# Splits of stored weight sums in place, and a changed order of small preparation jobs, in a fused attention and two-MLP kernel

## The chip, the core and the metric

The kernel runs as one program on one core of a Trainium2 chip. The metric is the device time of one execution in microseconds (us). Three timed runs of the kernel before gave 981.01, 981.85 and 983.27 us; the median is 981.85 us.

## The reference

```
scores = scale * q @ k^T - slope_h * |i - j|, masked to 0 <= i - j < 128
attn   = exp(scores - max) / (sum + 1e-9);  x = attn @ v        # 4 x 8 heads, 576 x 64
h = x @ w_in;  g = h * clip(h + 3, 0, 6) / 6;  x = g @ w_out    # 2304 x 512, 2048 features
xn = x / sqrt(mean(x^2) + 1e-6) * rms_g                         # second MLP, 1536 features
out = (silu(xn @ w_gate) * (xn @ w_val)) @ w_out2
```

The attention inputs and the output are float32. The weights are float64; the kernel gets them as 64-bit words and makes float32 of them itself.

## The kernel before, in words

Every float32 matrix is split into a rounded high part and the low rest, and a product is three matmuls (high by high, high by low, low by high). ScalarE (ACT) makes the high part with a copy, VectorE (DVE) the low part with a subtraction. A split is therefore an ACT instruction, then a DVE instruction that waits for it, and where the parts go to memory two stores.

The program has two halves. In the first (to about 533 us) attention and the first MLP run together in 6 blocks of 3 token tiles, 16 feature chunks each. Alongside, `Second.turn` (L269) converts the second MLP's weights in 36 turns, in the order of `TURNS` (L65): kinds 0 and 1 are the gate and value weights of a chunk, kind 2 is the output weight, of which each pair of chunks also gives two sums that go to memory as `sum32`, still unsplit.

In the second half 36 groups follow (`group`, L913): group i works on tokens of pair i // 12 and feature chunk i % 12. A group forms gate and value of its chunk by a scheme with seven products of six matmuls each, `product(0)` to `product(6)`, into three PSUM banks `ps_1`, `ps_6`, `ps_5`. Between them stand small instructions that read a bank before the next product may add to it:

- L938: ACT copies the first product to `s1`. `product(2)` adds to that bank, and waits until the copy is done.
- L941: DVE adds `s1` and `ps_6`. `product(3)` adds to `ps_6`, and waits for it.
- L944: ACT's silu of `ps_1`, after `product(2)`.
- L947: DVE adds `s1` and `ps_6` again; `product(5)` starts anew in `ps_6`, and waits for it.
- L950, L952, L956, L957: DVE's last adds and the multiplication.

Engines run their instructions in program order, with waits for each other. What is not part of a group's own chain is put between these by tables: `job(i, slot, ...)` hangs a piece of work on group i at a slot ("start" before `product(0)`, "silu" behind L944, "sum", "silu 2" behind the second silu, "end" behind L957, and numbers 0 to 5 behind the units of the output product that follow the group).

Groups 0 to 11 multiply their result by the output weights directly (`outputs`, L971, after groups 2, 4, 6, 8, 11 and 12). Groups 12 to 35 form six rounds of four groups. A round's output product is again one with seven factors (`Round`, L1038): its units run after groups 5, 6 and 7 counted from the round's first, so after groups 17, 18, 19 for round 0 (`phase`, L1121). DVE adds each unit's result to a total (L1135; in the first round of a token pair ACT copies it for some units, L1133). A unit of the names in `CHAINED` adds to the bank of an earlier unit, and waits until that unit's result was read. The operands of a round, B11, B12, B21, B22 and the sums T1 to T4 of the two chunk pairs p = 0 and 1, are made by `sum` (DVE, L1078), `high` (ACT, L1081) and `low` (DVE, L1084), where `ROUND_JOBS` (L75) says; the key is (group counted from the round's end, slot). `FINAL_JOBS` (L96) does it for the last round, which has no groups behind it.

The round's other factors are sums of output weights. `load_sum` (L301) loads one `sum32` piece of 128x512 into `ws`, `split_sum` (L305) splits it, and two stores put the parts back (L311); `Round.fetch` loads them as `u` (L1097) three factors ahead. Loads and stores, and `tw`, the operands of a later group (L889, two of 896 KB each at a group's end), are issued by the one queue of SyncE (SP), which waits in order.

The jobs of the pair of tokens after (`x.scale`, `x.later`, `x.high`, `x.low` in `turn`, L1176) go through the same slots.

Of the kernel before, what the change touches and what calls it, by code (L numbers as in the profile page):

```python
# [10 lines left out]
F32 = mybir.dt.float32  # L11
F32R = mybir.dt.float32r
# [8 lines left out]
P = 128  # L21
# [35 lines left out]
B11, T2, B21, T3, T1, T4, B22 = range(7)  # L57
# [4 lines left out]
PAIRS2 = NTILE // 6  # L62

ROUND = 4
TURNS = [(m + i, k) for m in range(0, M2, 2) for i, k in ((0, 2), (0, 0), (1, 2), (0, 1), (1, 0), (1, 1))]  # L65
FACTORS = {"c": ("S4", "B22"), "g": ("S3", "T3"), "a": ("A11", "B11"), "b": ("A12", "B21"), "e": ("S1", "T1"), "f": ("S2", "T2"), "d": ("A22", "T4")}
SEQUENCE = list(FACTORS)
STORED = {"A11": (0, 0, 0), "A12": (0, 1, 0), "A22": (0, 1, 1), "S2": (1, 0, 0), "S3": (1, 0, 1), "S4": (1, 1, 0), "S1": (1, 1, 1)}
ADDED_TO = {"c": "C12", "a": "V", "g": "C22", "b": "C11", "e": "V", "f": "V", "d": "Z"}
SUMMED = ["C11", "C12", "C22", "V", "Z"]  # L70
BLOCK_RING = (12, 10, 11)
SPLIT_AT = 5
OPERANDS = "B22 B11 B21 T3 T1 T2 T4".split()
CHAINED = {"b": "a", "d": "e"}
ROUND_JOBS = {  # L75
    (-1, "silu"): [("high", "B22", 0)],
    (-1, "silu 2"): [("low", "B22", 0)],
    (-1, 2): [("high", "B11", 0)],
    (-1, 3): [("low", "B11", 0)],
    (-1, 5): [("sum", "T1", 0)],  # L80
    (0, "start"): [("high", "B11", 1), ("high", "B22", 1), ("low", "B11", 1), ("sum", "T1", 1)],
    (0, "silu"): [("sum", "T3", 0), ("sum", "T3", 1), ("low", "B22", 1), ("high", "T3", 0), ("high", "T3", 1)],
    (0, "silu 2"): [("high", "B21", 0), ("high", "B21", 1)],
    (0, "end"): [("low", "T3", 0)],
    (1, "start"): [("low", "T3", 1)],
    (1, "silu"): [("sum", "T2", 0), ("sum", "T2", 1), ("low", "B21", 0)],
    (1, "silu 2"): [("low", "B21", 1)],
    (1, 2): [("high", "T1", 0), ("high", "T1", 1)],
    (1, 3): [("high", "T2", 0), ("high", "T2", 1), ("low", "T1", 0)],
    (2, "start"): [("low", "T1", 1), ("sum", "T4", 0)],  # L90
    (2, "silu"): [("low", "T2", 0), ("low", "T2", 1)],
    (2, "silu 2"): [("sum", "T4", 1)],
    (2, 3): [("high", "T4", 0), ("high", "T4", 1)],
    (3, "start"): [("low", "T4", 0), ("low", "T4", 1)],
}
FINAL_JOBS = {  # L96
    (-2, "start"): [("high", "B11", 0), ("high", "B21", 0), ("high", "B22", 0)],
    (-2, "silu"): [("low", "B11", 0)],
    (-2, "silu 2"): [("low", "B21", 0), ("low", "B22", 0)],
    (-2, "end"): [("sum", "T1", 0), ("sum", "T3", 0)],  # L100
    (-2, 3): [("sum", "T2", 0), ("sum", "T4", 0), ("high", "T3", 0), ("high", "T2", 0)],
    (-1, "silu"): [("low", "T3", 0), ("low", "T2", 0), ("high", "T1", 0), ("high", "T4", 0)],
    (-1, "silu 2"): [("low", "T1", 0)],
    (-1, "end"): [("low", "T4", 0), ("high", "B11", 1), ("high", "B21", 1), ("high", "B22", 1)],
# [8 lines left out]
}  # L113
UNITS = {5: "c0 c1 g0 g1".split(), 6: "a0 a1 b0 b1".split(), 7: "e0 e1 f0 f1 d0 d1".split()}

# [5 lines left out]
def f32(ap):  # L121
    return ap.bitcast(F32)
# [3 lines left out]
def fused_kernel(ctx: ExitStack, tc: tile.TileContext, qd, kd, v, w1, w2, rms_g, out, out_t):  # L126
# [7 lines left out]
    vec, act, pool, pe, sp = nc.vector, nc.scalar, nc.gpsimd, nc.tensor, nc.sync  # L134
# [105 lines left out]
    class Second:  # L240
# [109 lines left out]
    W1, W2 = First(), Second()  # L350
# [177 lines left out]
    def at(t):  # L528
        return [slots[kind].get(t, []) for kind in KINDS]
# [128 lines left out]
    for t in range(AHEAD):  # L658
        q, s_, d_, t_, _, v_ = at(t)
# [105 lines left out]
    for p, (b, m0, m1) in enumerate(PARTS):  # L765
# [3 lines left out]
        if p == 2:  # L769
            conv.close()  # L770
            ypool = ys.enter_context(tc.tile_pool(name="ypool", bufs=3, **OPEN))
        if last:
# [3 lines left out]
            ypool = p2.enter_context(tc.tile_pool(name="ypool2", bufs=3, **OPEN))  # L776
# [3 lines left out]
        for m in range(m0, m1):  # L780
# [48 lines left out]
            if p == 0:  # L829
                k = m + 1  # L830
# [18 lines left out]
            if last:  # L849
# [6 lines left out]
                for x in early:  # L856
                    k = m - EARLY[x.m]
# [48 lines left out]
    def job(i, at, f, *args):  # L906
        jobs.setdefault((i, at), []).append((f, args))
# [130 lines left out]
    class Round:  # L1038
# [70 lines left out]
        def plan(self, job):  # L1109

            i = self.i0 + ROUND
            if self.final:
                for at, jobs_ in FINAL_JOBS.items():
                    for f, *args in jobs_:
                        job(i + at[0], at[1], getattr(self, f), *args)
                return
            for at, jobs_ in ROUND_JOBS.items():
                for f, *args in jobs_:
                    job(i + at[0], "end" if self.r == 0 and at[0] < 0 and at[1] != "silu" else at[1], getattr(self, f), *args)
# [40 lines left out]
    for m, x in parts.items():  # L1160
        i = m - 2
# [14 lines left out]
    def turn(s):  # L1176

        i, x = s * M2, Inputs(s + 1)
        job(i + 5, "start", x.load)
        if s:  # L1180
            for c in range(KC):
                job(i + 6, ("silu", "end")[c // 2], x.scale, c, act)
            job(i + 7, "silu", x.later, "S1", 0)
            job(i + 7, 2, x.later, "S2", 1)
            job(i + 7, 2, x.high, 0)
            job(i + 7, 4, x.low, 0)
            job(i + 9, 3, x.later, "S4", 2)
            job(i + 9, 3, x.high, 1)
            job(i + 10, "silu 2", x.low, 1)
            job(i + 10, 3, x.later, "S3", 3)  # L1190
            for k in range(2, 7):
                job(i + 11, {2: "silu", 3: "sum", 5: "silu 2"}.get(k, "end"), x.high, k)
                job(i + 11, k - 1, x.low, k)
# [17 lines left out]
    for i in range(M2):  # L1211
        job(SPLIT_AT - 1 + i, "end", W2.load_sum, i)
        job(SPLIT_AT + i, "silu", W2.split_sum, i)

    for i in range(M2 * PAIRS2):
        s, m = divmod(i, M2)
# [17 lines left out]
        x = Round.all.get(i - ROUND)  # L1234
# [4 lines left out]
    x = rounds[-1]  # L1239
# [48 lines left out]
```

## Time and profile before

| | |
|---|---|
| timed runs | 981.01, 981.85, 983.27 us |
| the profiled execution | 985.32 us, its span 983.6 us |
| mean granted TensorE clock | 0.983 of full speed |
| busy: PE, DVE, ACT, POOL | 943.7, 696.0, 479.2, 220.4 us |
| DMA | 197.08 MB, mean 200 GB/s |

PE (TensorE) is busy for 96% of the span, so PE's idle stretches, and stretches at a lower granted clock, are what another order of the work can change. In the chain of work that ended last PE has 78%, DVE 10%, ACT 5% and DMA 3%.

The views used below: the timeline lists an engine's instructions with start, duration, line and tile, and in brackets the idle time before the first of them and what ended it. The chain goes from the end back to what released each step. The windows give busy time of PE, PEld, DVE, ACT and POOL in a stretch, then the granted clock, DMA share and GB/s.

### The profile page before, as it was taken

The page shows a single profiled execution, that of the slowest core. Times are in us where ns is not written, and L with a number is a line of the kernel's source. Part 1 is how long each engine was busy: PE and PEld are TensorE (multiplying, and loading weights), DVE is VectorE, ACT ScalarE, POOL GpSimd, SP SyncE. Part 2 cuts the span into 40 slices and gives each one's busy share as a digit, 9 for nine tenths or more (in the row PEclk, how much of TensorE's full clock was granted, in tenths as well). Part 3 has the DMA queues.
Part 4 walks back from the last instruction along what each step waited for, and adds up shares of the span by engine and source line. Part 5 has one row for each costly group of instructions (what it writes and reads, how often), then busy time and mean ns, then how long its engine had stood idle before and what let it go on. Part 6 is the DMA issues. An engine that isn't in the chain of part 4 may idle for free.

```text
span 983.6 us, 15380 instructions
## 1 busy us (share of the span) xinstructions
PE 943.7 (96%) x5408; PEld 845.7 (86%) x5408; DVE 696.0 (71%) x1464; ACT 479.2 (49%) x1049; POOL 220.4 (22%) x359
## 2 busy tenths in 40 slices
PE   7899999999999999999999997999989999999997
PEld 4577888888888888888899996889879998999986
DVE  5788666555888787876576664788465778685776
ACT  6799556355556556553454442433135333223420
POOL 4333013233334533433331332100000000020001
PEclk8899999999999999999999998999999999999999
DMA  6445411114775655542466778787979666777616
GB/s 234 175 182 197 172 38 31 41 52 129 241 235 179 204 184 171 199 161 93 143 230 218 269 249 308 257 291 254 310 283 339 233 236 214 251 267 253 230 53 207
DMA packets 96044, 197.08 MB, mean 200 GB/s; under 512 B 7008, under 2 KB 67424, under 8 KB 92768
## 3 DMA queue, kind: packets, MB, share of 16 engines
q1 hardware_dynamic: 95968, 196.11, 57.8%
q8 instruction: 42, 0.69, 0.3%
q14 instruction: 34, 0.28, 0.1%
HBM read 142.61 MB, written 53.48 MB: 199 GB/s over the span
## 4 chain that ended last, share of the span: by engine, by line
PE 78%; DVE 10%; ACT 5%; DMA 3%; issue 2%; POOL 1%; SPq 0%; ACTq 0%; DVEq 0%; POOLq 0%
PE ps_o L578 18%; PE ps_h L565 18%; PE ps_o L930 8%; PE ps_S L930 7%; PE ps_y L1104 7%; PE ps_A L930 5%; PE ps_y L980 5%; DMA ws<-s 3%; PE ps_av L499 3%; PE ps_h L930 3%; PE ps_t L481 2%; PE ps_s L438 2%; PE ps_s L429 1%; DVE wx L195 1%; ACT wx L188 1%
## 5 line engine op out<-in xcount | busy, mean ns | idle before, releaser
L578 PE MATMUL ps_o<-w,g 128*128 128x512 f32 x864 | 224.0, 402 | 2.1 <-DVE w L199 1.9
L565 PE MATMUL ps_h<-xs,w 128*128 128x384 f32 x1152 | 220.6, 339 | 0.0
L565 PEld LDWEIGHTS ps_h<-xs,w 128*128 128x128 f32 x1152 | 202.1, 188 | 6.7 <-DVE t L805 1.2
L578 PEld LDWEIGHTS ps_o<-w,g 128*128 128x128 f32 x864 | 156.2, 188 | 41.0 <-issue 6.1
L805 DVE SCALAR_TENSOR_TENSOR t<-t,ps_h 128x384 f32<-128x384 f32 x96 | 53.0, 552 | 87.2 <-ACT t L804 87.2
L804 ACT ACTIVATE t<-ps_h,three 128x384 f32<-128x384 f32 x96 | 55.5, 578 | 80.9 <-PE ps_h L565 74.7
L1104 PE MATMUL ps_y<-u 128*128 128x384 f32 x432 | 84.7, 337 | 1.9 <-DVE u L1135 1.7
L1151 POOL TENSOR_TENSOR u<-u 128x384 f32<-128x384 f32 x6 | 7.2, 1237 | 332.3 <-DVE u L1135 332.3
L1104 PEld LDWEIGHTS ps_y<-u 128*128 128x128 f32 x432 | 76.2, 189 | 2.9 <-DVE u L1135 2.5
L467 ACT ACTIVATE t<-t,m 128x128 f32<-128x128 f32 (+1 forms) x144 | 61.1, 426 | 29.4 <-DVE t L459 15.8
L810 ACT CAST g<-t 128x384 fp32r<-128x384 f32 x96 | 49.3, 514 | 53.2 <-DVE t L805 51.7
L816 DVE TENSOR_TENSOR g<-t,g 128x384 fp32r<-128x384 f32 x96 | 55.8, 581 | 23.1 <-ACT g L810 22.2
L953 ACT ACTIVATE r<-r 128x384 f32<-128x384 f32 x36 | 18.9, 526 | 106.0 <-DVE r L952 106.0
L469 POOL TENSOR_SCALAR r<-den 128x2 f32<-128x2 f32 x72 | 27.8, 387 | 182.8 <-ACT t L467 181.0
L930 PE MATMUL ps_o<-S,tw 128*128 128x384 f32 x336 | 66.7, 340 | 0.3 <-DVE t L950 0.3
L930 PEld LDWEIGHTS ps_o<-S,tw 128*128 128x128 f32 x336 | 58.9, 188 | 2.4 <-DVE u L941 1.6
L470 POOL TENSOR_TENSOR r<-r,minus 128x2 f32<-128x2 f32 x72 | 56.0, 778 | 6.0
L488 POOL TENSOR_SCALAR_AFFINE_SELECT pt<-pt 128x256 f32<-128x256 f32 x82 | 39.7, 487 | 76.6 <-ACT pt L486 73.7
L980 PE MATMUL ps_y<-wo,g 128*128 128x512 f32 x216 | 50.8, 394 | 0.0
L980 PEld LDWEIGHTS ps_y<-wo,g 128*128 128x128 f32 x216 | 41.3, 192 | 8.3
L452 DVE CUSTOM_DVE_ANT_0 t<-ps_s,rel 128x256 f32<-128x256 f32 (+2 forms) x128 | 45.1, 393 | 4.4 <-PE ps_s L438 4.4
L1081 ACT CAST u<-u 128x384 fp32r<-128x384 f32 x66 | 32.1, 512 | 30.2 <-DVE u L1078 14.3
(168 smaller groups left out, 1765.6 us busy)
## 6 DMA issues: line engine op xcount, KB each, us to landing
tw<-t SPq DMA_DIRECT2D x52, 896.0 KB, 6.5
wraw<-w SPq DMA_DIRECT2D x36, 512.0 KB, 4.3
wraw<-w SPq DMA_DIRECT2D x16, 1024.0 KB, 8.9
u<-s SPq DMA_DIRECT2D x48, 256.0 KB, 5.9
t<-th SPq DMA_DIRECT2D x12, 896.0 KB, 4.5
t<-tl SPq DMA_DIRECT2D x12, 896.0 KB, 4.3
u<-w SPq DMA_DIRECT2D x36, 256.0 KB, 5.4
w<-w SPq DMA_DIRECT2D x12, 512.0 KB, 2.9
```

Source lines behind the costliest of these rows:

```text
L452: vec.tensor_tensor_reduce(out=self.t[:, a, c0:], in0=s[:, c0:], in1=(rel_split if self.i in SPLITS else rel)[:, c0:], scale=2.0 ** (-8.0 ...
L467: act.activation(p, p, AF.Exp, bias=self.m[:, a : a + 1], scale=-1.0, accum_out=self.den[:, a : a + 1])
L470: pool.tensor_tensor(self.r, self.r, minus, ALU.pow)
L565: pe.matmul(ps[:, : n * P], lhsT=w[:, a, c * P : (c + 1) * P], rhs=xs[c][:, b, : n * P], start=(k == 0), stop=(k == 3 * KC - 1),)
L578: pe.matmul(o, lhsT=g[:, a, i * P : (i + 1) * P], rhs=w[:, b], start=(m == first and a == 0 and b == 0), stop=(m == last and a == 1),)
L804: act.activation(r[:, :nq], ps[:, :nq], AF.Relu, bias=three)
L805: vec.scalar_tensor_tensor(out=r[:, :nq], in0=r[:, :nq], scalar=6.0, in1=ps[:, :nq], op0=ALU.min, op1=ALU.mult)
L810: act.copy(g[:, 0, :nq], r[:, :nq])
L816: vec.tensor_sub(g[:, 1, :nq], r[:, :nq], f32(g[:, 0, :nq]))
L930: pe.matmul(ps, lhsT=w[a][:, k, c * P : (c + 1) * P], rhs=x[:, b, c], start=(start and j == 0), stop=(j == 5), skip_group_check=True,)
L980: pe.matmul(ps, lhsT=gs[i + k][:, a, t // 3, t % 3 * P : (t % 3 + 1) * P], rhs=wo[i + k][:, b], start=(k == 0 and a == 0 and b == 0), stop ...
L1104: pe.matmul(ps, lhsT=w[:, p, a, d * P : (d + 1) * P], rhs=self.part(name, p, b), start=(p == j == 0 and k not in CHAINED), stop=(p == 1 an ...
```

## The change

The order of turns differs for chunks 4, 5 and 8, 9. A weight sum is loaded at the start of the group before its split (it was at that group's end), into one of two fixed pairs of tiles, and the low part overwrites the loaded piece. The splits stand in groups 7 to 10 and 12 to 19 (they stood in groups 5 to 16). Most jobs of a round and of the last round stand at other slots.

```diff
-TURNS = [(m + i, k) for m in range(0, M2, 2) for i, k in ((0, 2), (0, 0), (1, 2), (0, 1), (1, 0), (1, 1))]
+TURN_ORDER = ((0, 2), (0, 0), (1, 2), (0, 1), (1, 0), (1, 1)), ((0, 0), (0, 1), (0, 2), (1, 0), (1, 2), (1, 1))
+TURNS = [(m + i, k) for m in range(0, M2, 2) for i, k in TURN_ORDER[m in (4, 8)]]
-SPLIT_AT = 5
+SPLIT_AT = (7, 8, 9, 10, 12, 13, 14, 15, 16, 17, 18, 19)
 ROUND_JOBS = {
...
-    (-1, 5): [("sum", "T1", 0)],
-    (0, "start"): [("high", "B11", 1), ("high", "B22", 1), ("low", "B11", 1), ("sum", "T1", 1)],
+    (-1, 5): [("sum", "T3", 0), ("high", "T3", 0)],
+    (0, "start"): [("high", "B11", 1), ("high", "B22", 1), ("sum", "T2", 0)],
...
 FINAL_JOBS = {
...
-    (-2, "silu 2"): [("low", "B21", 0), ("low", "B22", 0)],
-    (-2, "end"): [("sum", "T1", 0), ("sum", "T3", 0)],
+    (-2, "silu 2"): [("low", "B11", 0)],
...
         def load_sum(self, i):
-            self.late[i] = ypool.tile([P, DM], F32, tag="y", name="ws")
-            sp.dma_start(out=self.late[i], in_=self.sum32[i // 2][:, i % 2])
+            k = i % 2
+            if k not in self.late:
+                self.late[k] = tuple(
+                    ypool.tile([P, DM], F32, tag=tag, name=name, bufs=1 if tag == "yt" else 3)
+                    for tag, name in (("y", "ws"), ("yt" if k else "y", "wt"))
+                )
+            sp.dma_start(out=self.late[k][0], in_=self.sum32[i // 2][:, k])

         def split_sum(self, i):
-            x = self.late.pop(i)
-            high, low = (ypool.tile([P, DM], F32R, tag="y", name="wt") for _ in range(2))
-            act.copy(high, x)
-            vec.tensor_sub(low, x, f32(high))
-            for k, y in enumerate((high, low)):
-                sp.dma_start(out=self.sums[i // 2][:, i % 2, k], in_=f32(y))
+            x, high = self.late[i % 2]
+            act.copy(high.bitcast(F32R), x)
+            vec.tensor_sub(x.bitcast(F32R), x, high)
+            for k, y in enumerate((high, x)):
+                sp.dma_start(out=self.sums[i // 2][:, i % 2, k], in_=y)
...
-    job(SPLIT_AT - 1 + i, "end", W2.load_sum, i)
-    job(SPLIT_AT + i, "silu", W2.split_sum, i)
+    job(at_ - 1, "start", W2.load_sum, i)
+    job(at_, "silu", W2.split_sum, i)
```

Every engine has as many instructions as before, and PE's are in the same order. Three places show what moves. The first is SP's queue around groups 13 and 14, before:

```order
L1097 DMA u<-w_1_130 128x2x256
L311 DMA s_4_139<-wt 128x512 x2
L303 DMA ws<-s_4_145 128x512
L889 DMA tw<-t_121 128x1792 x2
L311 DMA s_4_139<-wt 128x512 x2
L303 DMA ws<-s_5_146 128x512
L889 DMA tw<-t_122 128x1792 x2
```

and of the change, where `ws` is a load, `s<-wt` and `s<-ws` the stores of a split:

```order
L1109 DMA u<-w_1_130 128x2x256
L316 DMA ws<-s_3_144 128x512
L323 DMA s_2_137<-wt 128x512
L323 DMA s_2_137<-ws 128x512
L901 DMA tw<-t_121 128x1792 x2
L316 DMA ws<-s_3_144 128x512
L323 DMA s_3_138<-wt 128x512
L323 DMA s_3_138<-ws 128x512
L901 DMA tw<-t_122 128x1792 x2
```

The load stood between a group's stores and its `tw` pair. It now stands behind the `tw` pair of the group before and ahead of the stores.

The second is ACT around the start of group 24 (first group of a round), before; `u` and `S` rows of L1081 are `high` pieces, the `s` row is the copy of the first product:

```order
L754 CAST S_8554<-sums 128x768
L1081 CAST u<-u 128x384 x2
L1081 CAST S_7175<-u 128x384
L938 COPY s_8623<-ps_h 128x384
L944 ACTIVATE r<-ps_h 128x384
L1081 CAST u<-u 128x384 x2
```

and of the change (12 is added to the line numbers):

```order
L766 CAST S_8524<-sums 128x768
L1093 CAST u<-u 128x384 x3
L1093 CAST S_7155<-u 128x384
L950 COPY s_8593<-ps_h 128x384
L956 ACTIVATE r<-ps_h 128x384
L965 ACTIVATE r<-r 128x384
```

One more `high`, that of T3 for p = 0, stands ahead of the copy. The same holds at the starts of groups 16, 20, 28 and 32.

The third is DVE at the end of group 34, before; the L1078 rows are sums, L1084 `low` pieces, L1135 the adds of the units' results:

```order
L952 TENSOR_TENSOR r<-u,ps_A 128x384
L1078 TENSOR_TENSOR u<-u 128x384
L1084 TENSOR_TENSOR u<-u 128x384 x2
L956 TENSOR_TENSOR u<-u,ps_S_9616 128x384
L957 TENSOR_TENSOR u<-u,r 128x768
L1078 TENSOR_TENSOR u<-u 128x384 x2
L1135 TENSOR_TENSOR u<-u,ps_y 128x384 x4
```

and of the change:

```order
L964 TENSOR_TENSOR r<-u,ps_A 128x384
L1096 TENSOR_TENSOR u<-u 128x384
L968 TENSOR_TENSOR u<-u,ps_S_9584 128x384
L969 TENSOR_TENSOR u<-u,r 128x768
L1147 TENSOR_TENSOR u<-u,ps_y 128x384 x3
```

Four of the five jobs between L952 and the first L1135 stand elsewhere.

## Rows read from the trace of the kernel before

**Rows 1.** PE's timeline, second half (one row first half): waits stand in brackets
```profile
611.12 1.01 PE L930 MATMUL ps_A<-A,th 128*128 128x384 f32 x2 [6.52 <-DVE u L947]
640.01 0.69 PE L930 MATMUL ps_A<-A,th 128*128 128x384 f32 x2 [2.49 <-DVE u L947]
689.20 1.32 PE L930 MATMUL ps_A<-A,tw 128*128 128x384 f32 x6 [0.17 <-DVE u L947]
714.29 1.33 PE L930 MATMUL ps_A<-A,tw 128*128 128x384 f32 x6 [1.44 <-DVE u L947]
727.52 1.33 PE L930 MATMUL ps_h<-A,tw 128*128 128x384 f32 x6 [0.54 <-ACT s L938]
729.65 1.32 PE L930 MATMUL ps_A<-S,tw 128*128 128x384 f32 x6 [0.80 <-DVE u L941]
823.73 1.47 PE L930 MATMUL ps_A<-S,tw 128*128 128x384 f32 x6 [1.97 <-DVE u L941]
944.16 0.68 PE L1104 MATMUL ps_y<-A,u 128*128 128x384 f32 x1 [1.96 <-DVE u L1135]
963.73 8.62 PE L1104 MATMUL ps_y<-u 128*128 128x384 f32 x48 [1.74 <-DVE u L1135]
322.20 0.44 PE L481 MATMUL ps_t<-ident,t 128*128 128x128 f32 x2 [0.48 <-ACT pt L486]
```

**Rows 2.** The chain of waits around group 6: start, duration, what
```profile
597.89 11.28 DMA ws<-s
...
611.12 2.29 PE ps_A L930 x6
613.41 1.92 PE ps_S L930 x6
615.33 8.83 PE ps_y L980 x36
```

**Rows 3.** The same chain elsewhere: paces at full and at lower clock
```profile
582.61 8.18 PE ps_y L980 x36
...
640.01 1.97 PE ps_A L930 x6
641.99 1.92 PE ps_S L930 x6
...
734.18 2.10 PE ps_S L930 x12
...
944.16 3.92 PE ps_y L1104 x12
```

**Rows 4.** Windows of 10 us; granted clock is the third number from the end
```profile
610.00:620.00 10.00, 8.88 (x31) 7.95 (x32) 6.11 (x9) 5.97 (x8) 2.88 (x4) 0.67 0.49 171
710.00:720.00 10.00, 8.56 (x49) 8.24 (x48) 4.67 (x8) 2.26 (x5) 0.00 (x0) 1.00 0.97 350
820.00:830.00 10.00, 8.03 (x37) 7.71 (x37) 6.93 (x14) 2.38 (x6) 0.00 (x0) 0.83 0.30 101
```

**Rows 5.** ACT's timeline in group 8 and at the start of group 20
```profile
638.15 0.62 ACT L308 CAST wt<-ws 128x512 fp32r<-128x512 f32 x1 [1.28 <-DMA ws<-s]
773.05 0.93 ACT L1081 CAST u<-u 128x384 fp32r<-128x384 f32 x2
```

**Rows 6.** DVE's timeline at the starts of groups 16, 24 and 28
```profile
725.58 0.96 DVE L957 TENSOR_TENSOR u<-u,r 128x768 f32<-128x768 f32 x1
820.26 0.55 DVE L1135 TENSOR_TENSOR u<-u,ps_y 128x384 f32<-128x384 f32 x1
869.66 1.25 DVE L1078 TENSOR_TENSOR u<-u 128x384 f32<-128x384 f32 x1
```

**Rows 7.** DMA issues, 530 to 760 us: count, KB each, median us to landing
```profile
tw<-t SPq DMA_DIRECT2D x24, 896.0 KB, 6.9
s<-wt SPq DMA_DIRECT2D x24, 256.0 KB, 4.2
ws<-s SPq DMA_DIRECT2D x12, 256.0 KB, 4.9
```

More of the change, by code (lines that the diff above doesn't have):

```diff
@@ L75 @@
 ROUND_JOBS = {
-    (-1, "silu"): [("high", "B22", 0)],
-    (-1, "silu 2"): [("low", "B22", 0)],
+    (-1, "start"): [("high", "B22", 0)],
+    (-1, "silu"): [("low", "B22", 0)],
     (-1, 2): [("high", "B11", 0)],
     (-1, 3): [("low", "B11", 0)],
-    (-1, 5): [("sum", "T1", 0)],
-    (0, "start"): [("high", "B11", 1), ("high", "B22", 1), ("low", "B11", 1), ("sum", "T1", 1)],
-    (0, "silu"): [("sum", "T3", 0), ("sum", "T3", 1), ("low", "B22", 1), ("high", "T3", 0), ("high", "T3", 1)],
-    (0, "silu 2"): [("high", "B21", 0), ("high", "B21", 1)],
+    (-1, 4): [("sum", "T1", 0)],
+    (-1, 5): [("sum", "T3", 0), ("high", "T3", 0)],
+    (0, "start"): [("high", "B11", 1), ("high", "B22", 1), ("sum", "T2", 0)],
+    (0, "silu"): [("low", "B11", 1), ("sum", "T1", 1), ("low", "B22", 1)],
+    (0, "silu 2"): [("sum", "T3", 1), ("high", "T3", 1)],
     (0, "end"): [("low", "T3", 0)],
-    (1, "start"): [("low", "T3", 1)],
-    (1, "silu"): [("sum", "T2", 0), ("sum", "T2", 1), ("low", "B21", 0)],
+    (1, "start"): [("sum", "T2", 1), ("high", "B21", 0), ("high", "B21", 1)],
+    (1, "silu"): [("low", "T3", 1), ("low", "B21", 0)],
     (1, "silu 2"): [("low", "B21", 1)],
+    (1, "end"): [("sum", "T4", 0)],
+    (1, 0): [("sum", "T4", 1)],
     (1, 2): [("high", "T1", 0), ("high", "T1", 1)],
-    (1, 3): [("high", "T2", 0), ("high", "T2", 1), ("low", "T1", 0)],
-    (2, "start"): [("low", "T1", 1), ("sum", "T4", 0)],
+    (1, 3): [("low", "T1", 0)],
+    (2, "start"): [("low", "T1", 1), ("high", "T2", 0), ("high", "T2", 1)],
     (2, "silu"): [("low", "T2", 0), ("low", "T2", 1)],
-    (2, "silu 2"): [("sum", "T4", 1)],
     (2, 3): [("high", "T4", 0), ("high", "T4", 1)],
@@ L97 @@
     (-2, "start"): [("high", "B11", 0), ("high", "B21", 0), ("high", "B22", 0)],
-    (-2, "silu"): [("low", "B11", 0)],
-    (-2, "silu 2"): [("low", "B21", 0), ("low", "B22", 0)],
-    (-2, "end"): [("sum", "T1", 0), ("sum", "T3", 0)],
[L101 to L104, printed above, removed]
[8 rows of a table removed]
+    (-2, "silu 2"): [("low", "B11", 0)],
+    (-2, 2): [("low", "B21", 0)],
+    (-2, 3): [("low", "B22", 0), ("sum", "T1", 0)],
+    (-1, "silu"): [("sum", "T3", 0), ("sum", "T2", 0), ("sum", "T4", 0), ("high", "T3", 0)],
+    (-1, "silu 2"): [("low", "T3", 0)],
+    (-1, "end"): [("high", "B11", 1), ("high", "B21", 1), ("high", "B22", 1)],
+    (-1, 0): [("low", "B11", 1)],
+    (-1, 1): [("low", "B21", 1)],
+    (-1, 2): [("low", "B22", 1)],
+    (-1, 3): [("sum", "T1", 1)],
+    (-1, 4): [("sum", "T3", 1), ("high", "T3", 1)],
+    (-1, 5): [("sum", "T2", 1)],
+    (2, 1): [("low", "T3", 1), ("high", "T1", 0), ("high", "T1", 1)],
+    (2, 2): [("sum", "T4", 1)],
+    (2, 3): [("low", "T1", 0), ("high", "T2", 0), ("high", "T2", 1)],
+    (1, 0): [("low", "T1", 1)],
+    (1, 1): [("low", "T2", 0)],
+    (1, 2): [("low", "T2", 1), ("high", "T4", 0), ("high", "T4", 1)],
+    (1, 3): [("low", "T4", 0)],
+    (3, 0): [("low", "T4", 1)],
 }
@@ L1118, in plan @@
                 for f, *args in jobs_:
-                    job(i + at[0], "end" if self.r == 0 and at[0] < 0 and at[1] != "silu" else at[1], getattr(self, f), *args)
+                    job(i + at[0], {2: "silu", 3: "silu", 4: "silu 2", 5: "end"}.get(at[1], at[1]) if self.r == 0 and at[0] < 0 else at[1], getattr(self, f), *args)
         def phase(self, off, by):
@@ L1192, in turn @@
                 job(i + 11, {2: "silu", 3: "sum", 5: "silu 2"}.get(k, "end"), x.high, k)
-                job(i + 11, k - 1, x.low, k)
+                job(i + 11, {2: "silu 2", 3: "end"}.get(k, k - 3), x.low, k)
             return
@@ L1210, in fused_kernel @@
         x.plan(job)
-    for i in range(M2):
-        job(SPLIT_AT - 1 + i, "end", W2.load_sum, i)
-        job(SPLIT_AT + i, "silu", W2.split_sum, i)
+    for i, at_ in enumerate(SPLIT_AT):
+        job(at_ - 1, "start", W2.load_sum, i)
+        job(at_, "silu", W2.split_sum, i)
     for i in range(M2 * PAIRS2):
```

8 rows, old and new, of the table FINAL_JOBS are left out of this document.

## The prediction

> **What bounds the kernel now.** I read the page's busy shares first: PE is busy for 943.7 of 983.6 us. PE's program is the same after the change, so the change can only take away or add PE's idle stretches, and stretches at a lower clock. Next I read who PE waits for, and then PE's timeline [rows 1], where the reader is to see that the waits of the second half fall into three sorts. One is L947 behind a split of a weight sum: 6.52 us in group 6, 2.49 in group 8, 1.44 in group 14. One is the first group of a round (0.54 and 0.80 in group 16, 1.97 in group 24). One is the last round (1.96 after group 34, 1.74 after group 35). The chain [rows 2] shows what lies behind the first: the load of a weight sum takes 11.28 us to land, ACT's copy waits for it, DVE's subtraction waits for ACT, and L947 stands behind that subtraction in DVE's order. The windows [rows 4] show what follows a long wait: the granted clock of the window with the 6.52 us is 0.67, of the one with the 1.97 us 0.83, that is time at 1.2 instead of 2.4 GHz; with the 1.44 us it is 1.00. The price is in the chain: twelve matmuls after the 6.52 us take 2.29 + 1.92 us [rows 2], at full clock 2.10 [rows 3].
>
> **The splits of the weight sums.** No instruction is added: a split is still one ACT copy, one DVE subtraction of the same shape and two stores. The load moves from a group's end to its start.
> - Group 6 has no split any more. The wait of 6.52 goes, the slow twelve matmuls give back 2.29 + 1.92 - 2.10 = 2.11, the slow output product 8.83 - 8.18 = 0.65 [rows 2, 3]. Sum 9.28.
> - Group 8 keeps a split. Of its 2.49 us only the 1.28 that ACT waited for the load goes [rows 5]; the rest is ACT's larger copy ahead of the split, which stays. A wait of 1.21 is shorter than the 1.44 that kept the full clock [rows 1, 4], so the slow stretch goes too: 1.97 + 1.92 - 2.10 = 1.79 [rows 3]. Sum 3.07.
> - Group 14: 1.44 less the 0.17 that a split costs PE even when its load is there [rows 1]. Sum 1.27.
> - Groups 17, 18 and 19 get a split that they did not have: 3 x 0.17 = 0.5 lost.
>
> What is late next? The load now stands behind the `tw` pair in SP's queue, and it overwrites a tile whose two stores must have landed. In the short groups 13 to 16 a group takes 12 + 30 matmuls, 7.35 us at the pace of [rows 3] (2.10 for 12). The split comes after three products of the next group and L944, some 3.5 us into it, so the load has about 10.9 us from the start of its group. Against that stand the `tw` pair's landing of 6.9 us and, for the reused tile, stores that take 4.2 us to land [rows 7] and leave about 3 us before the start. The load should land 8 to 9 us after the start: in time, with little to spare, so I charge 0.7 us. Behind a load that waits for stores stand the stores of the next split and then the next `tw` pair; `tw` is needed two groups, 14.7 us, after its request and lands in 6.9, so a delay of a few us there is hidden. The parts are fetched for round 0 behind group 12, and the splits that it needs end in group 10, so the later splits cost nothing. The part as a whole: 9.28 + 3.07 + 1.27 - 0.5 - 0.7 = 12.4 us gained. From the other side, were every load as late as before, only group 6 would gain.
>
> Here the Trainium skill speaks against the change (DMA: Bandwidth & Descriptors, section "Queues, rings and completion order"): descriptors are consumed in ring order, so a load issued behind two 896 KB transfers starts behind them. By its peak of 436 GB/s the pair alone would take 4.2 us, an estimate from that page; the trace has 6.9 us to landing [rows 7]. By that rule the load loses its place at the front, and that is the first rival below.
>
> **The rounds.** DVE loses work at the starts: ahead of L941 the T2 sum stands in place of a `low` and the T1 sum. But ACT gets one more `high`, that of T3, ahead of the copy `s1` for which `product(2)` waits, and this `high` waits for a DVE sum that was only just placed behind the last add of the phase. A `high` takes 0.41 us in a row (two in 0.93, less the tail) [rows 5], `s1` 0.48.
> - Group 16: L957 ends at 725.58 + 0.96 = 726.54 [rows 6]. The T3 sum follows (0.47), then three `high` (1.24) and `s1` (0.48) with some 0.1 of signals: 728.8. `product(2)` was ready at 727.52 - 0.54 = 726.98 [rows 1]. Wait 1.85 against 0.54 + 0.80 now: 0.5 lost.
> - Group 24: DVE is behind here. Its last add of the phase starts at 820.26 [rows 6]. In the new order one `low` of the next operands (0.95, of which 0.87 until the next) and the T1 sum (0.47) come ahead of it and one copy's rest (0.58) leaves, so 821.0; the T3 sum ends at 822.0, and three `high` and `s1` give 823.8. `product(3)` could have started at 823.73 - 1.97 = 821.76 [rows 1], `product(2)` one product (1.05) earlier, at 820.7. Wait 3.1 against 1.97: 1.1 lost.
> - Group 28: the sum runs beside GpSimd there and takes up to 1.25 instead of 0.55 [rows 6]; a wait of 1.0 to 1.7 in place of one of that size: 0.1 lost.
> - Groups 20 and 32 (ACT copies the last units itself, the DVE sum is early): one more `high`, 0.41 less a slack of 0.3: 0.1 to 0.2 each; the B22 `high` ahead of `s1` in 19 and 31 likewise 0.1 each. Together 0.5.
> - Clock: the waits of groups 16 and 24 lie at or above those followed by a slow stretch; group 24 has one already [rows 4]. I charge a third of 1.79 for group 16: 0.6.
> Sum: 0.5 + 1.1 + 0.1 + 0.5 + 0.6 = 2.8 lost. Bounds: nothing lost and the 0.54, 0.80 and half of 1.97 gained (2.3), or each of the five starts as bad as group 24 (below).
>
> On group 28 the Trainium skill (SBUF — State Buffer, "Who interferes with whom") says that a VectorE instruction with two SBUF inputs and a GpSimd instruction that reads SBUF block each other for whole instructions. The sum is of that kind, and 1.25 us against 0.55 agrees. [...]
>
> **The last round.** After group 34 the unit b waits for the add of unit a, which waits for DVE: five jobs stand between L952 and that add, and four of them leave. L956 then starts when PE's product ends, L957 after it (0.96 [rows 6]), the add ends about 2.3 us after the product, and the third unit can start after 2.10 [rows 3]: a wait of about 0.25 instead of 1.96. Gain 1.7, and the slow twelve matmuls 3.92 - 2.10 = 1.82 [rows 3]. After group 35 each add has one job beside it now (0.47 + 0.47 per unit of 1.05), so DVE keeps up and the 1.74 goes. Sum 5.3. Later units need their operands at least three units after the jobs, so nothing is late there. Bounds: 1.96 + 1.82 + 1.74 = 5.5 gained; or, if a job lands one unit late twice, 2.1 less.
>
> **The turns** move instructions in the first half only. PE has two waits there that hang on them (the first stands in [rows 1], 0.48, the other is under 0.7). A conversion of kind 2 stays in that place, so I take 0, bounds plus and minus 1.2.
>
> **The sum.** 12.4 - 2.8 + 5.3 = 14.9 us. Against the profiled execution of 985.32 us that is 970.4; that one is 3.5 us above the median, and against the median of 981.85 it is 967.0 us.
>
> **Rivals.**
> 1. The loads stay late, since they stand behind `tw` and wait for stores. For it: the DMA share is 0.97 in the window of group 14 [rows 4]. Against it: the request comes over 2 us earlier even after the stores. Then groups 13 to 16 wait 1.3 us each as group 14 did (5.2) and group 8 keeps its slow stretch (1.8): 974.0.
> 2. Slower side: the `high` of T3 ahead of `s1` decides at all five starts. It needs DVE to be as far behind at each as in group 24; for it, ACT's order; against it, DVE has gaps before the others. Each start then costs 3.1 plus a slow stretch of 1.8 to 2.8 as after 6.52 us, 4.9 to 5.9; five are 24.5 to 29.5, less today's 5.1 (0.54, 0.80, 1.97, 1.79): 19.4 to 24.4 in place of 2.8. The time is 983.6 to 988.6. It decides from 4.6 us per start.
> 3. The load that lands after 11.28 us belongs to the profiled execution, which is 3.5 us longer than the median. Then 3.5 less is gained: 970.5.
> 4. Those heads of rounds hide in PE's running ahead, and the T3 cost is nought: 962 to 964.
>
> **How the numbers follow.** Forecast 0.55, rival 1 0.15, rival 2 0.05, rival 3 0.10, rival 4 0.12, unknown 0.03. The range reaches from rival 4, with 3 us for the turns and what I did not see, to rival 1, with 2 more: 959 to 976. About 0.2% (2 us) is what a measurement can tell. Faster 0.93, same 0.03, slower 0.04.
>
> **What would show it.** Right: no wait at L947 over 0.6 us but in group 8, ACT not waiting for `ws`, no slow stretch near groups 6, 8 and 34, and a wait of PE for ACT's `s1` at groups 16, 24 and 28 that was 0.54 us at one place before. Wrong: ACT waits for `ws` in groups 13 to 16, waits for `s1` over 3 us at more than one round, or new waits for `tw`.

## The result, and the profile after

The changed kernel takes 970.8 us (median of 6 runs, 969.73 to 974.01); the kernel before took 982.66 us beside it (6 runs, 981.01 to 986.07). The ratio is 0.9879, interval 0.9856 to 0.9902: 11.9 us, or 1.2%, faster. The forecast was 967.0 us in a range of 959 to 976.

The profiled execution took 970.52 us (span 968.8, mean clock 0.992); before it was 985.32 us. PE is busy for 937.8 us in place of 943.7. PE's timeline after, at the places of [rows 1], start, duration, what, and in brackets the wait:

```profile
628.19 0.63 PE L942 MATMUL ps_A<-A,th 128*128 128x384 f32 x2 [2.04 <-DVE u L959]
700.91 1.32 PE L942 MATMUL ps_A<-A,tw 128*128 128x384 f32 x6 [0.17 <-DVE u L959]
715.42 1.32 PE L942 MATMUL ps_h<-A,tw 128*128 128x384 f32 x6 [1.84 <-ACT s L950]
752.49 1.32 PE L942 MATMUL ps_o<-A,tw 128*128 128x384 f32 x6 [1.03 <-DVE u L959]
764.12 1.32 PE L942 MATMUL ps_h<-A,tw 128*128 128x384 f32 x6 [0.92 <-ACT s L950]
812.52 1.83 PE L942 MATMUL ps_h<-A,tw 128*128 128x384 f32 x6 [3.09 <-ACT s L950]
860.38 1.32 PE L942 MATMUL ps_h<-A,tw 128*128 128x384 f32 x6 [1.31 <-ACT s L950]
```

The 6.52 us of group 6 and both waits of the last round (1.96 and 1.74) have no row any more. Behind groups 34 and 35 the output products now begin and run on without a wait in brackets:

```profile
932.90 0.44 PE L1116 MATMUL ps_y<-A,u 128*128 128x384 f32 x1
942.59 14.73 PE L1116 MATMUL ps_y<-u 128*128 128x384 f32 x84
```

What is left of waits over 0.6 us is that of group 8 (2.49 before) and five at the starts of rounds and in group 19, four of them for ACT's copy `s1`. The list of waits (430 to 970 us; who waits for whom: us in total, times, longest) puts that copy on top:

```profile
PE ps_h L942 <- ACT s L950: 7.3, 5, 3.1
PE ps_A L942 <- DVE u L959: 2.7, 5, 2.0
PE ps_o L942 <- DVE u L959: 2.0, 4, 1.0
```

To lay the two traces side by side I took the start of `s1` in each group (the COPY rows `s<-ps` of ACT) and added up the stretches, in us (the first relu is ACT's first instruction on a result of the first MLP):

| stretch | before | changed | difference | foretold |
|---|---|---|---|---|
| start to the first relu | 42.79 | 40.38 | -2.4 | 0 |
| first relu to group 4 (turns) | 533.59 | 534.42 | +0.8 | 0 |
| group 4 to 15 (splits) | 141.43 | 129.62 | -11.8 | -12.9 |
| group 15 to 34 (rounds, splits in 17 to 19) | 216.22 | 220.25 | +4.0 | +3.3 |
| group 34 to PE's end (last round) | 44.90 | 39.46 | -5.4 | -5.3 |

The profiled difference of 14.8 us meets the foretold 14.9 by chance: 2.4 us of it lie before the first relu, where both programs have the same instructions in the same order. In a second profile of the changed kernel (below) and in those of its variants this stretch took 40.4 to 42.3 us; what sets it is open. From the first relu on the difference is 12.4, which agrees with the 11.9 that the runs give.

### The profile page after: what moved, and what is told of

It is laid out like the page before. It is cut to its first block, busy times and chain, and to the rows that moved or that the text cites. A ratio compares the mean times of both kernels' runs of the same rounds, so it can differ in the third digit from the quotient of the medians.

```text
span 968.8 us, 15365 instructions
## 1 busy us (share of the span) xinstructions
PE 937.8 (97%) x5408; PEld 840.3 (87%) x5408; DVE 692.6 (71%) x1464; ACT 478.5 (49%) x1049; POOL 217.4 (22%) x359
## 4 chain that ended last, share of the span: by engine, by line
PE 73%; DVE 11%; ACT 7%; DMA 4%; issue 3%; POOL 2%; SPq 0%; ACTq 0%; POOLq 0%; DVEq 0%
PE ps_o L590 18%; PE ps_h L577 18%; PE ps_o L942 8%; PE ps_S L942 6%; PE ps_y L1116 5%; PE ps_A L942 4%; PE ps_y L992 4%; PE ps_h L942 3%; PE ps_av L511 2%; DMA tx<-b 2%; DMA tw<-t 1%; PE ps_t L493 1%; DVE u L1147 1%; ACT t L479 1%; DVE wx L203 1%
## 5 line engine op out<-in xcount | busy, mean ns | idle before, releaser
L479 ACT ACTIVATE t<-t,m 128x128 f32<-128x128 f32 (+1 forms) x144 | 61.2, 426 | 29.4 <-DVE t L471 14.9
L500 POOL TENSOR_SCALAR_AFFINE_SELECT pt<-pt 128x256 f32<-128x256 f32 x82 | 36.9, 452 | 81.9 <-ACT pt L498 79.0
```

Of the source, the lines that this page charges most:

```text
L479: act.activation(p, p, AF.Exp, bias=self.m[:, a : a + 1], scale=-1.0, accum_out=self.den[:, a : a + 1])
```

## The experiments

Tables give stretches as above, from one profile of each kernel; times and ratios are those of the timed runs, each against runs of the kernel before on the same chip.

### The four parts alone

**Splits.** The kernel before with `load_sum`, `split_sum`, `SPLIT_AT` and the two jobs of the change, and nothing else of it:

```diff
+    job(at_ - 1, "start", W2.load_sum, i)
+    job(at_, "silu", W2.split_sum, i)
```

> The kernel before with the in-place splits, the earlier loads and the new places of the splits alone. My theory: the stretch from group 5 to 7 gets 9.3 to 9.8 us shorter, group 8 only about 0.5 us (its larger ACT copy waits for GpSimd's sums of a tile that DMA brings late, in place of the load), group 14 about 1.3 us, group 19 loses 0.9 us because a DVE sum of the next tokens stands behind the split. In all 10 to 11.5 us faster, 971 to 972.5. Rival (the loads stay late behind the two large transfers): ACT waits for the loaded piece in groups 13 to 16, about 1.3 us each, and the gain is 5 to 7 us.

Measured: 973.54 us (4 runs), ratio 0.9893 (0.9873 to 0.9913). From the first relu on the profile is 9.9 us shorter: group 4 to 15 is 13.4 shorter, group 15 to 34 2.5 longer, 2.1 of it in groups 18 and 19, and the stretch behind group 34 1.2 longer, where this kernel has no edit. Group 8 is 2.0 us shorter and not 0.5, since no slow stretch follows its wait here. So the splits carry most of the result, and the ones put into 17 to 19 cost five times the 0.5 that I had charged.

**Rounds.** Only `ROUND_JOBS` and what hangs on it:

```diff
+    (-1, 5): [("sum", "T3", 0), ("high", "T3", 0)],
+    (0, "start"): [("high", "B11", 1), ("high", "B22", 1), ("sum", "T2", 0)],
```

> The kernel before with the new places of a round's jobs alone (and of the pair's low parts in group 23). My theory: PE waits for ACT's copy of the first product at the starts of groups 16, 20, 24 and 28, about 1.8, 0.9, 3.1 and 1.3 us, in place of waits at L941 and one of 0.54; in all 2 to 4 us slower than before. Rival (the spread of the sums pays): the waits at L941 go and nothing takes their place, 3 to 5 us faster.

Measured: 984.73 us (10 runs), ratio 1.0015 (0.9999 to 1.003). Group 15 to 34 is 3.2 us longer, group 34 to the end 2.1 shorter. There T4's sum has left the place in front of the chained unit, which takes the wait of 1.96 us to 1.50:

```profile
943.89 0.44 PE L1106 MATMUL ps_y<-A,u 128*128 128x384 f32 x1 [1.50 <-DVE u L1137]
```

The other 1.6 us are the slow stretch, which does not follow this wait. Group 4 to 15, where this kernel has no edit until group 15, is 2.4 shorter, also without a shorter wait in groups 6 and 8 (6.77 and 2.69). By itself the part gains nothing.

**Last round.** Only `FINAL_JOBS`:

```diff
+    (-1, "silu"): [("sum", "T3", 0), ("sum", "T2", 0), ("sum", "T4", 0), ("high", "T3", 0)],
+    (-1, "silu 2"): [("low", "T3", 0)],
```

> The kernel before with the new places of the last round's jobs alone. My theory: the wait of 1.96 us after group 34 goes with its slow stretch of 1.8 us, and the wait of 1.74 us after group 35 goes: 5.3 us faster, the whole of it after group 34. Rival (the jobs only move the lateness to later units): 1.5 to 3 us faster, with new waits of PE for DVE in the last 15 us.

Measured: 979.62 us (5 runs), ratio 0.9964 (0.9949 to 0.9979), 3.5 us faster. Group 34 to the end takes 40.48 in place of 44.90, 4.4 less. Of the wait of 1.96 us 0.44 is left, that of 1.74 is gone, and near the end there is one of 0.76 us for the load `u<-s`. It need not come from this part: the run with the splits alone, whose last round is as before, has one of 0.78, and the changed kernel has none.

```profile
941.33 0.44 PE L1109 MATMUL ps_y<-A,u 128*128 128x384 f32 x1 [0.44 <-DVE u L1140]
966.52 0.41 PE L1109 MATMUL ps_y<-A,u 128*128 128x384 f32 x1 [0.76 <-DMA u<-s]
```

**Turns.** Only `TURN_ORDER`:

```diff
+TURN_ORDER = ((0, 2), (0, 0), (1, 2), (0, 1), (1, 0), (1, 1)), ((0, 0), (0, 1), (0, 2), (1, 0), (1, 2), (1, 1))
```

> The kernel before with the new order of turns alone. My theory: the waits of 0.48 and 0.67 us in the first half are replaced by two of 0.7 to 0.8 us for GpSimd's power; the first half gets 0.2 to 0.6 us longer, no difference in the time beyond noise. Rival (the new order frees ACT in the first half): 1 us faster. The difference of 2.4 us that the profiled executions showed before 43 us should not follow this edit, since the program is the same there.

Measured: 982.09 us (10 runs), ratio 0.9984 (0.9972 to 0.9996). The stretch that the part touches, first relu to group 4, is 0.6 us longer: the two waits for ACT of 0.48 and 0.67 us are exchanged for two for POOL, 0.4 us more. The rest is not the turns', as far as is known: the run of the rounds, which has no edit in this half, is 0.6 us longer there too.

```profile
335.09 1.53 PE L500 MATMUL ps_av<-pt,vraw 128*64 128x128 f32 x24 [0.72 <-POOL r L471]
419.35 1.53 PE L500 MATMUL ps_av<-pt,vraw 128*64 128x128 f32 x24 [0.80 <-POOL r L471]
```

The runs say 1.6 us faster. The profile has less time in group 6 (1.2), group 8 (1.6) and behind group 34 (1.3), and 0.8 more in group 10; this kernel has no edit in any of them. The waits are not shorter, they are 6.56, 2.42 and 1.97 us. What is missing is slow matmuls behind them, some in group 6 and all in group 8 and behind group 34. Behind group 34 the first matmul takes 0.44 us where it took 0.68 [rows 1], and the first twelve take 2.2 us in place of 3.92 [rows 3]:

```profile
609.91 1.01 PE L931 MATMUL ps_A<-A,th 128*128 128x384 f32 x2 [6.56 <-DVE u L948]
940.88 0.44 PE L1105 MATMUL ps_y<-A,u 128*128 128x384 f32 x1 [1.97 <-DVE u L1136]
```

So single profiles of kernels with the same waits can lie 4 us apart. Whether the order of turns has a part in that is open. By the runs the four parts alone add up to some 14 us faster, the change has 11.9; with four intervals of 1.2 to 2 us on either side that is no contradiction.

### What made the gain in group 6: the early load or the later split

The changed kernel with the loads requested late again:

```diff
-        job(at_ - 1, "start", W2.load_sum, i)
+        job(at_ - 1, "end", W2.load_sum, i)
```

> The changed kernel, with the load of each weights' sum requested at the end of the group before its use's group's predecessor, as it was in the kernel before, instead of at its start; the splits stay in place and where the change puts them. My theory: the place of the split made the gain of 9.3 us in group 6, and the earlier request adds only some margin: 1.3 to 4 us slower than the changed kernel, with waits of ScalarE at the split for the load in a few groups, the one of 1.3 us in group 14 among them. Rival: the early request made the gain; then group 6 is long again (about 24 us in place of 15.6) and it is 8 us or more slower.

Measured: 975.87 us (4 runs), ratio 0.9914 (0.9892 to 0.9937), against 0.9879 and 0.9884 in the two measurements of the changed kernel: some 3 to 3.5 us slower (the intervals just overlap). Group 6 keeps its 15.5 us (24.82 before). What returns is ACT's wait for the load, in groups 8 and 14 alone:

```profile
629.04 0.62 ACT L320 CAST wt<-ws 128x512 fp32r<-128x512 f32 x1 [1.64 <-DMA ws<-s]
703.12 0.62 ACT L320 CAST wt<-ws 128x512 fp32r<-128x512 f32 x1 [1.22 <-DMA ws<-s]
```

and PE's behind it:

```profile
630.90 0.62 PE L942 MATMUL ps_A<-A,th 128*128 128x384 f32 x2 [4.01 <-DVE u L959]
704.98 1.32 PE L942 MATMUL ps_A<-A,tw 128*128 128x384 f32 x6 [1.50 <-DVE u L959]
```

So the new places of the splits are enough for group 6's gain, since no split stands in it; the earlier request keeps 3.3 us in groups 8 and 14. Earlier requests with the splits left where they stood were not run.

### Group 8: what was next

Of the 3.07 us foretold there 0.47 came. The chain of waits of the changed kernel shows why; start, duration, what:

```profile
613.62 8.44 DMA tx<-b
...
624.01 1.34 POOL tx L340
625.36 0.02 issue
625.38 1.05 ACT th L347
626.43 0.53 ACT wt L320
626.96 0.02 issue
626.98 0.69 DVE ws L321
627.67 0.48 DVE u L959
628.15 0.04 issue
628.19 1.82 PE ps_A L942 x6
630.02 1.92 PE ps_S L942 x6
```

ACT's larger copy stands ahead of the split and waits for GpSimd's sums, and these wait for their own load. The copy's row in ACT's timeline of group 8, after and before:

```profile
625.38 1.05 ACT L347 CAST th<-tx 128x1024 fp32r<-128x1024 f32 x1 [0.81 <-POOL tx L340]
```

```profile
635.83 1.04 ACT L335 CAST th<-tx 128x1024 fp32r<-128x1024 f32 x1
```

Before, it followed the silu at once. My 1.21 us for "the rest" plus 0.81 make 2.02; the trace has 2.04. Group 8 now comes 11.4 us sooner, and the load `tx` is requested 11.0 us sooner (613.62 against 624.60) and takes 8.4 us to land in place of 7.9: GpSimd's first sum started 0.76 us ahead of `s1` before (632.63 against 633.39) and starts 0.18 behind it now (622.19 against 622.01). The test puts that copy behind the split:

```diff
-            job(i, "silu", x.high, 0)
+            job(i, "sum" if i == 8 else "silu", x.high, 0)
```

> The changed kernel, with the high part of the tenth chunk's first piece in group 8 moved from ahead of the split of the weights' sum to behind it. My theory: the wait of 2.04 us for u in group 8 is the split's, which stands in ScalarE's queue behind that high part, which waits for GpSimd's sum, which waits for the load tx<-b. Then the wait falls to about 0.2 us and the slow matmuls behind it (1.8 us each six in place of about 1.3) go too: 2.5 to 3.6 us faster than the changed kernel. Rival: the load of the weights' sum itself has not landed by then; then ScalarE waits at the split's own line for a DMA, and the gain is under 1 us.

Measured: 968.98 us (4 runs), ratio 0.9852 (0.9831 to 0.9874). Group 8 takes 16.36 us in place of 19.42, 3.1 less; about half of it wait (2.04 to 0.52) and half slow matmuls. By the runs it is some 3 us less than the changed kernel, with overlapping intervals. The split does not wait for its load, and the matmuls behind the rest of the wait run at full clock (granted 1.00 from 627 to 637 us):

```profile
627.66 0.62 PE L942 MATMUL ps_A<-A,th 128*128 128x384 f32 x2 [0.52 <-DVE u L959]
```

### The starts of rounds: ACT's `high` of T3, or DVE's backlog

```diff
-    (-1, 5): [("sum", "T3", 0), ("high", "T3", 0)],
+    (-1, 5): [("sum", "T3", 0)],
+    (0, "sum"): [("high", "T3", 0)],
```

> The changed kernel, with ScalarE's high part of T3's first piece moved from the end of group 15 (19, 23, 27) to behind the copy of s1 of the next group. My theory: the waits of TensorE for s1 (0.92 to 3.09 us in groups 16, 20, 24 and 28) are ScalarE's, which has that high part, itself waiting for VectorE's sum, ahead of the copy. Then the copy starts as soon as its matmuls are done: group 16 from 1.84 to about 0.5 us, group 20 from 0.92 to 0 to 0.3, group 24 from 3.09 to at most 1.2, group 28 from 1.31 to about 0.4; in all 4.5 to 7 us faster than the changed kernel (about 964 to 966 us). Rival: VectorE's own backlog at the group's turn decides; then the same lengths come back as waits for VectorE's add of u at L953 or L959 in the same groups, and the gain is under 1.5 us.

In the changed kernel at group 24 the two copies ahead of `s1` wait for DVE, and `s1` comes right behind (ACT's timeline):

```profile
810.76 0.92 ACT L1093 CAST u<-u 128x384 fp32r<-128x384 f32 x2 [6.99 <-DVE u L1090]
811.59 0.51 ACT L1093 CAST S<-u 128x384 fp32r<-128x384 f32 x1
812.00 0.47 ACT L950 COPY s<-ps_h 128x384 f32<-128x384 f32 x1
```

Measured: 964.59 us (4 runs), ratio 0.9812 (0.9784 to 0.984), 6 to 7 us less than the changed kernel. The rounds' starts (group 15 to 17, 19 to 21, 23 to 25, 27 to 29) fall by 1.3, 1.2, 3.4 and 0.3 us. At groups 24 and 28 part of the wait comes back at DVE's adds, as the rival says: 1.29 of 3.09 us, and 0.21 + 0.66 of 1.31 (lines here are one higher):

```profile
714.60 1.33 PE L943 MATMUL ps_h<-A,tw 128*128 128x384 f32 x6 [0.55 <-ACT s L951]
809.77 1.32 PE L943 MATMUL ps_A<-S,tw 128*128 128x384 f32 x6 [1.29 <-DVE u L954]
854.98 1.33 PE L943 MATMUL ps_A<-S,tw 128*128 128x384 f32 x6 [0.21 <-DVE u L954]
858.02 1.32 PE L943 MATMUL ps_A<-A,tw 128*128 128x384 f32 x6 [0.66 <-DVE u L960]
```

So ACT's order makes 4.5 of the 7.2 us of these waits, DVE's backlog the rest, at group 28 two thirds. A slow stretch of 1.5 us behind group 24's wait goes as well.

### Towards a version that beats both

Four moves together: the two copies of the last two runs, T3's first sum behind `s1` as well, and DVE's `later("S1")` out of group 19's "silu", where it stands between the split and the add that PE waits for:

```profile
750.41 0.69 DVE L321 TENSOR_TENSOR ws<-ws,wt 128x512 fp32r<-128x512 f32 x1 [1.36 <-ACT wt L320]
751.02 0.95 DVE L742 TENSOR_TENSOR sums<-x2raw 128x768 f32<-128x768 f32 x1
751.89 0.55 DVE L959 TENSOR_TENSOR u<-s,ps_o 128x384 f32<-128x384 f32 x1
```

```diff
+    (0, "sum"): [("sum", "T3", 0), ("high", "T3", 0)],
...
-            job(i + 7, "silu", x.later, "S1", 0)
+            job(i + 7, "silu 2", x.later, "S1", 0)
```

> The changed kernel with four moves: VectorE's sum and ScalarE's high part of T3's first piece both behind the copy of s1, the high part in group 8 behind the split, and VectorE's later sum of S1 in group 19 moved behind the add of u. By my theory, group by group against the changed kernel: group 16 1.3 us less, group 19 1.1, group 20 0.9, group 24 up to 4, group 28 0.8, group 8 3.0 to 3.6; in all 9 to 12 us faster, some 959 to 962 us. By the rival of VectorE's backlog the sums that were moved only stand ahead of the adds of u in place of the copy, and the gain is that of groups 8 and 19 alone, 3 to 5 us.

Measured: 960.41 us (4 runs), ratio 0.9761 (0.9737 to 0.9784). In this kernel T3's first sum reads a block after T2's has overwritten it, so that operand holds other values; instructions, shapes and their number are unchanged. Against the changed kernel groups 18 to 20 are 2.0 us shorter, group 8 3.3, and the starts of groups 16, 24 and 28 1.3, 3.9 and 0.6. The next run sets the order of the two sums right:

```diff
-    (0, "start"): [("high", "B11", 1), ("high", "B22", 1), ("sum", "T2", 0)],
+    (0, "start"): [("high", "B11", 1), ("high", "B22", 1)],
-    (0, "sum"): [("sum", "T3", 0), ("high", "T3", 0)],
+    (0, "sum"): [("sum", "T3", 0), ("sum", "T2", 0), ("high", "T3", 0)],
```

> The changed kernel with the moves of the run before it in which four were made, and T2's first sum moved too, from group 16's start (20, 24, 28) to right behind T3's first sum, which reads the block that T2's overwrites. My theory: VectorE's and ScalarE's queues hold nothing that is late in front of s1, and the time is that of the run with four moves: 959 to 961.5 us, 11 to 12.5 us less than the changed kernel. Rival: T2's sum stands in front of the add of u in groups 16, 20, 24 and 28 now, some 0.55 to 1.25 us each, where T3's stands already; then waits at L953 or L959 of that length come there, and it is 2 to 4 us slower than that run, 962 to 965 us.

Measured: 961.88 us (4 runs), ratio 0.9789 (0.977 to 0.9808): 21 us less than the kernel before, 9 less than the change. The time lies 0.4 us above the expected range and just below the rival's. From the first relu on it is 1.7 us longer than the run with four moves. Of the rival's waits at L953 and L959 the longest is 0.51 us, in group 28, and no wait above 0.6 us is left in the second half; still group 15 to 34 is 1.4 us longer, at most 0.3 in one group. Another 1.1 lie behind group 34, where PE waits 0.44 us for `u<-s`; the first half is 0.7 shorter. This was not followed up.

Two more on the same chip. The splits and the last round without rounds and turns (`load_sum`, `split_sum`, `SPLIT_AT`, `FINAL_JOBS` of the change; the rest as before):

```diff
+SPLIT_AT = (7, 8, 9, 10, 12, 13, 14, 15, 16, 17, 18, 19)
...
+    (-1, "silu"): [("sum", "T3", 0), ("sum", "T2", 0), ("sum", "T4", 0), ("high", "T3", 0)],
```

> The kernel before with the splits in place and their earlier requests, and the last round's jobs of the change; the rounds' sums of g and the order of the turns are those of before. My theory: the two parts give 9.9 and 4.4 us, and the spread sums and the turns gave nothing: 967.5 to 970.5 us, level with the changed kernel or up to 2 us faster. Rival: the parts need each other (the split of group 19 stands better between the spread sums): then 971.5 us or more, slower than the changed kernel.

and the changed kernel unaltered:

> The changed kernel once more, on the same chip as the two above, to compare with them: 969.5 to 972 us; and a second profile, in which the time before the first relu should differ (it lay between 40.4 and 42.8 us in the profiles so far), while the waits for s1 (0.92 to 3.09 us in groups 16, 20, 24 and 28) should stand as they were.

Measured: 968.37 us (5 runs), ratio 0.9856 (0.9831 to 0.988), and 970.9 us (5 runs), ratio 0.9884 (0.9865 to 0.9904). The intervals overlap, so by the runs the half that is left out costs 2.5 us or nothing; the rival, that the parts need each other, is out. The profiles have 3.1 us between them in group 15 to 34, 0.7 in the first half, and the other way 0.5 behind group 34. About half of the 3.1 is a slow stretch at group 24: the splits alone have the same order in that stretch and took 218.74 us, 1.5 less than the changed kernel. The second profile of the changed kernel repeats every wait listed under the result to 0.02 us, and its first relu comes at 40.44 us, not at another time as expected.

## Why the prediction was right, and where not

- **What bounds it** held: from the first relu on, all that was found to change lies in PE's waits and in slow stretches behind them. Of the signs that I named, ACT does not wait for `ws`, PE waits for `s1` at groups 16, 24 and 28, and no slow stretch is left near groups 6 and 34; but group 8 keeps one, and L959 has a wait over 0.6 us in group 19 too.
- **Splits, group 6**: 9.28 foretold, 9.25 measured. **Group 14**: 1.27 foretold, 1.28 measured. My reserve of 0.7 for late loads was not needed: no split waits for its load in the changed kernel. That settles rival 1: the loads take longer to land, 6.8 us against 4.9 before [rows 7], but they are asked for earlier by more. Two rows of the DMA issues after (count, KB each, median us to landing):

```profile
tw<-t SPq DMA_DIRECT2D x26, 896.0 KB, 6.6
...
ws<-s SPq DMA_DIRECT2D x12, 256.0 KB, 6.8
```

  A load asked for right behind a `tw` pair (656.65 us, the pair's second at 656.18) lands 6.8 us later, behind the pair. This agrees with the Trainium skill (DMA: Bandwidth & Descriptors, "Queues, rings and completion order"), by which a DMA engine consumes descriptors in ring order. It decided nothing here.
- **Splits, group 8**: the step that failed. "The rest is ACT's larger copy ahead of the split, which stays" took the copy's time for a constant. The copy waits for GpSimd's sums and these for a load, which came 10.4 us sooner when its group came 11.4 us sooner; so the wait fell by 0.45 us and not by 1.28. The other term, 1.79 for the slow stretch, I had taken from the length of the wait. It stayed in both profiles of the changed kernel, yet with the splits alone it did not follow a wait of 2.07, nor with the turns alone one of 2.42. In all 0.47 came instead of 3.07, and moving the copy gave the other 3.1.
- **Groups 17 to 19**: 0.17 each was foretold. Group 14's and 18's waits are 0.17, group 19's is 1.03, since I did not look at what else stands in DVE's order between the split and the add. It is L742, 0.95 us: with that sum moved (the run with four moves) the wait is 0.17.
- **Rounds**: waits of 1.85, 3.1 and 1.0 to 1.7 us were foretold for groups 16, 24 and 28; 1.84, 3.09 and 1.31 are there. Group 20 has 0.92, not 0.1 to 0.2: a `low` of DVE for the next tokens (L770, 0.95 us) stands ahead of T3's sum (the first of L1090's two), as DVE's timeline after has it:

```profile
760.90 0.95 DVE L770 TENSOR_TENSOR A<-x2raw,A 128x768 fp32r<-128x768 f32 x1
761.77 1.15 DVE L1090 TENSOR_TENSOR u<-u 128x384 f32<-128x384 f32 x2
```

  The working also left out 0.81 us that PE waits at L947 in group 16 before; the change takes it to 0.17. The slow stretch that I charged to group 16 did not come (1.00 in that window). The part's total, foretold as 2.8, lies between 1.5 (group 15 to 34 of the changed kernel against the splits alone) and 3.2 (rounds alone).
- **Last round**: 5.3 foretold, 5.4 between the two profiles. 1.82 of it is the slow stretch behind 1.96 us, which the turns alone do not have behind 1.97; the part alone is 3.5 us faster by its runs. So the waits were right, and the exact agreement is in part luck.
- **Turns**: 0 foretold; the first half is 0.6 to 0.8 us longer, inside the bounds, of which 0.4 can be put to the exchanged waits.
- **The base.** I carried the working of a profiled execution over to the median unchanged. The time, 970.8, is nearest rival 3's 970.5, but not for its reason. It took the late load of group 6 for a mark of the one profiled execution; yet with the rounds, the last round and the turns alone, which leave group 6 as it was, that load lands after 11.5, 11.4 and 11.3 us too, and PE waits 6.77, 6.69 and 6.56 us, in profiled executions of 983.57, 979.60 and 981.77 us. What the profiled execution has above the median is not shown; its 42.79 us to the first relu are the longest of all profiles.
- **The slow stretches** are 6.4 us of the 14.9 foretold (2.11 + 0.65, 1.79 and 1.82), and the profile before has them in full. With the turns alone, behind the same waits, 4 us of such time is missing. So group 6's 9.25 us and the last round's 5.4 hold for this pair of profiles; against the profile of the turns alone they are 8.1 and 4.1.

Foretold from the first relu on 14.9, measured 12.4: 1.1 are the splits (group 8's 2.6 less what other places gave), 0.7 the rounds with group 19, 0.8 the first half.

## What to carry to other kernels

When a long wait is taken away, work behind it comes sooner, and loads need not come sooner by as much (here 10.4 us against 11.4): list them, and look at the first consumer of each. A wait that you read as the time of one instruction can be that instruction's own wait for something else. A copy that frees a bank for the matmuls should have nothing in its engine's queue ahead of it that waits for another engine; here moving one 0.41 us copy behind it at the starts of five rounds gave some 6 us, the slow stretch of 1.5 us among them. For a split that is moved to a new slot, read the slot's whole queue on the second engine too, not the slot's usual price.

## What was not expected of the hardware

A wait of one length is followed by a slow stretch in some profiles and not in others. Group 24 begins with a wait of 3.09 us both in the changed kernel and in the one with late requests. In the first, six matmuls take 1.83 us behind it (the timeline under the result), and the granted clock of 810 to 820 us is 0.83:

```profile
810.00:820.00 10.00, 7.48 (x34) 7.48 (x35) 5.77 (x12) 3.02 (x7) 0.00 (x0) 0.83 0.17 56
```

(busy PE, PEld, DVE, ACT, POOL, then granted clock, DMA share, GB/s). In the other they run at full speed:

```profile
817.70 1.32 PE L942 MATMUL ps_h<-A,tw 128*128 128x384 f32 x6 [3.09 <-ACT s L950]
818.86 1.22 PE L942 MATMUL ps_A<-S,tw 128*128 128x384 f32 x6
```

At group 16 it is the other way about: behind 1.84 us of wait the changed kernel goes on at 1.32 us for six matmuls, the one with group 8's copy moved does not:

```profile
713.37 2.19 PE L942 MATMUL ps_h<-A,tw 128*128 128x384 f32 x6 [1.84 <-ACT s L950]
```

And behind group 8's wait, 2.04 us in the changed kernel and 2.07 with the splits alone, the windows read, in this order:

```profile
630.00:640.00 10.00, 10.00 (x43) 8.57 (x42) 8.18 (x12) 1.98 (x3) 0.00 (x0) 0.89 0.73 267
```

```profile
630.00:640.00 10.00, 10.00 (x48) 8.58 (x47) 9.25 (x14) 2.02 (x4) 0.00 (x0) 1.00 0.78 259
```

Each such stretch costs 1.1 to 1.6 us (group 15 to 17: 19.37 against 18.28; 23 to 25: 26.11 against 24.56; 8: 19.42 against 17.88). I had foretold them from the length of the wait alone; in these rows it does not decide. Two profiles of kernels with equal waits can differ by that much at each such place, so waits are compared first. What does decide is open: the two profiles of the changed kernel agree at groups 8, 16 and 24, which speaks for the kernel, while the mean granted clock of its first six runs lies between 0.987 and 0.994, which speaks for the execution.
